# Two more dummy matmuls before the gate's transposition, the gate weights as one load, and new orders on all engines

## The chip, the core and the metric

The kernel runs on one core of one Trainium2 chip. Its engines work side by side, each through its own list of instructions in a fixed order: TensorE (PE, matmuls; PEld is its loading of weights), VectorE (DVE), ScalarE (ACT), GpSimd (POOL) and SyncE (SP, which here only issues DMAs). They wait for each other through semaphores. The metric is the time of one execution in device microseconds, as the median of several runs.

## The reference

Two branches work on the same input x of 2048 rows and 448 columns (the second branch ignores its own input), and a gate per row mixes them.

```python
g = sigmoid((x * gate_w).sum(-1))                  # one number per row
# A: attention, 16 heads of 28, four segments of 512 rows, causal within a segment,
#    plus a linear memory of the segments before (phi(t) = t+1 for t>0, else exp(t))
q, k, v = x@wq, x@wk, x@wv
o = sigmoid(beta) * (phi(q)@M)/(phi(q)@z + 1e-6) + (1-sigmoid(beta)) * softmax(q k^T * scale + mask) @ v
a = o @ wo
# B: an MLP over the rows
h = layernorm(x)
u = gelu(einsum("bsd,sf->bdf", h, w1) + b1)        # 1792 wide
b = transpose(einsum("bdf,fs->bds", u, w2) + b2)
out = g*a + (1-g)*b
```

## The kernel before

All five engines get their work from one list of operations with dependences (`Sched`). The order in which each engine takes them does not come from the program text but from a table, `ORDER`: one string of names for each engine, in which `u1-3*2` stands for two operations (step 3 and 4 of MLP group 1) and `@5` for the PSUM bank or buffer that an operation takes. `plan` only replays these strings. So an engine whose next operation isn't ready holds back everything behind it in its string, SP's DMA issues too.

The stages, in the names of the table:

- Loads. SP issues x transposed in four blocks of 512 rows (`dtx0_0` for the first three column groups, `dtx0_1` for the fourth), the weights of K and Q (`ldwk`, `ldwq`), x in rows in four pieces (`ldx0`, `ldx4`, `ldx8`, `ldx12`), beta, and the MLP weights in quarters (`ldw1_0_0` and so on). ACT's queue issues V's weights (`ldwv`), the gate's weights (`ldgw`, `ldgwb`), the last quarter of K's and the biases.
- Start of PE. `warm` is a run of dummy matmuls on ones (L626) that nothing reads. `gtr` (L810) transposes the gate's weights, which lie as rows in the zeroed `gstage`, into a column by a matmul with columns of the identity; DVE copies the column beside V's weights (`gw`, L812), so that the V projection makes the gate's sum as its 449th column. `warm2` is one more dummy. Then come V's projections of the first block (`pra`, `prb`, `lot`, `prt`: the four column groups of 128 rows of weights; the fourth overlaps the third, and its new half is done as a pair of half-row matmuls, `lo`), then K's and Q's (`pra0_`, `lok`, `prk`, `prx`, `loq`, `prq`). K's weights go through DVE first, which spreads 28 columns of a head to 32 (`padk`, `padx`, L637). `btr` (L857) transposes the biases.
- Copies out of PSUM (`cpv` L790/L792, `cpk` L706/L708, `cpq` L766/L768, `gt` L793 for the gate), on ACT or DVE as the table says.
- Layernorm on DVE: `bns` (L882, statistics of one tile of 128 rows), `bna` (L884), `vpe` (L889), `rstd` on POOL (L891), `nmr` (L893), `ln` (L898, the normalised tile).
- Attention: 40 score groups `sc` (L939) into the four PSUM banks 0 to 3, each followed by one exponential over all four on ACT (`exp`, L948); the next group can start only when the exponential has read the banks. POOL masks, `pv` (L975) multiplies with V, and DVE transposes and combines.
- MLP: `u0-0` to `u13-15` (first matrix, 16 steps over the row tiles; step t of any `u` reads `ln` of tile t and a quarter of `w1`), gelu in `gsq`, `gvh`, `garg`, `gth`, `gelu`; `y0-0` to `y15-13` (second matrix). `wo` is the output projection, `ag` its copy with the gate, `fin` (L1079) the mix, `out` the store. PE uses the `u` and `y` steps to fill the time between score groups. Most matmuls of L264 run either as one of 128 columns of weights or as four of 32 side by side.

The four banks 4 to 7 serve everything else; `@` in PE's string says which.

The dummies and the gate before:

```python
warm_up(7, "warm", -1)
warm_up(1, "warm2", P_PROJ + 0.01, 3500.0)
```

Of the kernel before, what the change touches and what calls it, by code (L numbers as in the profile page):

```python
# [5 lines left out]
ACT = mybir.ActivationFunctionType  # L6
# [12 lines left out]
NCT = 4  # L19
# [260 lines left out]
def pool_cost(n):  # L280
# [7 lines left out]
warm gtr@4 warm2 pra0@5 pra1@6 pra2@7 pra3@4 prb3 prb2 prb0 prb1 lot2 lot0 prt1 prt3 prt2 prt0 pra0_1 pra0_2 pra0_0  # L288
btr@5 lok0_0 lok0_2 prk0_0 prx0_3 prk0_2 prk0_1 loq1_2@74 loq1_0@65 prq1_2h prq1_1 prq1_2 prq1_0 loq0_0 lok1_0@57
prk1_1 prq0_0 loq0_2 lok1_2@64 prk1_0 prx1_3 prk1_2 prq0_2 prq0_2h prq0_1 lot4@75 lot6@46 prt7 prt6 prt4 prt5 sc0_0  # L290
lok2_2@64 prx2_3 u1-0@7 u0-0@5 u1-1 prk2_2 u1-2 u0-1 u1-3*2 u0-2*4 u1-5 sc0_1 lok2_0@46 prk2_1 u1-6*2 prk2_0
u2-0@6*2 sc0_2 u2-2 u0-6 u2-3 u1-8*2 u0-7 u2-4 u0-8*3 u2-5 sc0_3 u1-10 u0-11*3 u2-6 u0-14 u1-11 u0-15 u2-7*2 u1-12
u2-9 sc0_4 u1-13 u2-10 u1-14 u2-11 u4-0@4*2 u1-15 u4-2 pv0@5 u4-3 sc1_0 u2-12 u4-4 u2-13 u3-0@5*2 u2-14 u4-5 u3-2
u4-6 u3-3*2 u2-15 pv1@7 u3-5*2 u4-7 u3-7 sc1_1 u4-8*2 u3-8 u4-10 u6-0@7 u5-0@6 u4-11 u5-1 u6-1*2 u3-9 u4-12*3 u3-10
u4-15 u3-11 u6-3*3 sc1_2 u3-12*2 u5-2 u6-6*2 u3-14 u7-0@4 u3-15 u6-8*4 u5-3 u7-1 u6-12*4 u7-2 sc1_3 u5-4 u7-3*2
u5-5*3 u8-0@5 u5-8*2 u7-5 u8-1 u5-10*3 u7-6 sc1_4 u8-2 u7-7 u5-13 u8-3 pv2@7 u7-8 u8-4 u5-14 u8-5 u7-9 u5-15 u7-10
sc2_0 u8-6 mst0@7 u8-7*3 u7-11 u8-10 u9-0@6 u8-11 u9-1 sc2_1 u8-12*2 u9-2 u8-14*2 u9-3 pv3@7 u9-4 u7-12*2 u9-5
u7-14 u9-6 u7-15 u9-7 sc2_2 loq2_0@75 u9-8*2 prq2_1 u9-10*2 prq2_0 sc2_3 loq2_2@45 prq2_2 u9-12*2 wo2@7 u9-14
prq2_2h u9-15 sc2_4 mem4@4 wo0#1@7 wo3@5 pv4@6 wo1@4 sc3_0 lot8@75 prt9 u10-0@6*2 prt8 u10-2*2 sc3_1 u10-4*2 mem5@4
pv5@5 u10-6*5 sc3_2 u10-11 u11-0@4 u10-12 u11-1 u10-13*3 mst1@5 u11-2*4 sc3_3 lot10@75 u11-6*3 prt11 u11-9 prt10  # L300
u13-0@6 sc3_4 u11-10*2 mem6@5 u13-1 u11-12 pv6@7 u11-13 u13-2 u12-0@5 u11-14*2 u13-3 sc4_0 u12-1 u13-4*3 u12-2
u13-7*2 mem7@7 u13-9 u12-3*2 u13-10 sc4_1 u12-5 u13-11*2 pv7@4 u13-13*2 u12-6 u13-15 u12-7*3 sc4_2 lok3_0@74
u12-10*3 prk3_0 u12-13*3 prk3_1 sc4_3 lok3_2@67 prx3_3 prk3_2 loq3_0@45 prq3_0 sc4_4 prq3_1 wo6@6 wo7@7 sc5_0 wo5@4
wo4@6 pv8@7 y2-0@5*2 sc5_1 y2-2 y1-0@4 y2-3*2 y1-1 pv9@6 y2-5 y1-2 mem8@7 sc5_2 y1-3 y2-6 y1-4 y0-0@6 y1-5*3 y2-7
y0-1 y1-8 mem9@7 sc5_3 y0-2*3 y1-9 y2-8 y1-10 y0-5 y2-9 y0-6 y4-0@7 y2-10 y1-11 y4-1 y0-7 sc5_4 y2-11*2 y0-8 y2-13
y1-12*2 y4-2 y0-9*3 y5-0@5 y0-12 y5-1 y4-3 sc6_0 y4-4 mem10@4 y5-2 y4-5*2 y5-3 y0-13 y5-4*2 y4-7 y5-6*3 sc6_1 y4-8
pv10@4 y5-9*2 mem11@6 y5-11*3 y4-9 y3-0@4 sc6_2 y4-10 y3-1 y4-11 y3-2 y4-12*2 pv11@6 y3-3*2 sc6_3 lot14@57 y3-5
prt15 y3-6 mst2@6 prt14 y3-7*2 sc6_4 loq3_2@67 prq3_2 y3-9 prq3_2h y6-0@5 y3-10*2 y6-1 y3-12 lot12@67 sc7_0 y3-13
prt12 prt13 y6-2*3 mem12@4 sc7_1 y6-5 wo10@6 y6-6 wo8@4 pv12@7 y8-0@6 y6-7 y8-1*3 wo11@4 y8-4 mem13@7 y6-8 y8-5
sc7_2 y6-9 pv13@4 y7-0@7 y6-10 y8-6*2 y6-11*3 y8-8*2 mem14@4 sc7_3 y8-10 y7-1*2 wo9@5 pv14@4 y7-3 sc7_4 y7-4 y9-0@5  # L310
y8-11*3 y9-1 y7-5 y9-2 y11-0@4 y7-6 y9-3*2 y7-7 y9-5 y7-8 y9-6 y7-9 y9-7 y7-10 y9-8 pv15@6 y11-1 y7-11*2 y9-9*3
mem15@6 y11-2*6 y7-13 y9-12*2 y10-0@6*4 y11-8 y10-4*4 y11-9 y10-8*3 y11-10*4 y10-11*3 wo12@7 wo15@5 wo13@6 wo14@4
y13-0@7*2 y12-0@5 y13-2 y12-1 y15-0@6 y12-2*2 y14-0@4*2 y12-4 y13-3*2 y12-5*3 y14-2*4 y12-8 y13-5 y15-1 y14-6 y15-2
y14-7*3 y13-6*2 y14-10 y15-3*2 y14-11 y15-5*2 y13-8*3 y14-12 y13-11 y12-9 y14-13 y12-10 y15-7 y13-12*2 y15-8 y12-11
# [892 lines left out]
```

## Time and profile before

| | us |
|---|---|
| median of 3 runs (lowest, highest) | 173.28 (172.91, 173.67) |
| the profiled execution, as timed | 173.6 |
| its span, first to last instruction | 171.9 |
| PE busy | 167.2 |
| DVE busy | 143.9 |
| ACT busy | 128.0 |
| POOL busy | 61.5 |

The page of the profile gives busy time by engine and the chain of work that ended last; the timeline gives instructions in order of time, equal neighbours merged into one row (start, duration from the first start to the last end, count, and in brackets the idle time before and what ended it). A matmul's duration has the time in it that its results need to come out, so that neighbours overlap; how fast PE runs is read from the distance of the starts, or from the count in a stretch (the windows view: stretch, its length, PE's busy time and count, granted clock, DMA share, GB/s). The DMA view gives, for the issues in a stretch, the time from issue to landing.

### The profile page before, as it was taken

The numbers are of one execution on the slowest core, as the hardware profiler recorded it, in microseconds if no ns is written. First come the engines' busy times: TensorE is split into PE (matmuls) and PEld (weight loads), VectorE is DVE, ScalarE is ACT, GpSimd is POOL, SyncE is SP. The second block draws the span as 40 slices with busy tenths as digits, with TensorE's granted clock in tenths as the row PEclk, the third lists the DMA queues.
The fourth block names the chain that finished last, engine by engine and source line by source line (L and its number), as shares of the span: only waits on it lengthen the run. The fifth ranks groups of instructions, "written<-read, shape, count | busy, mean of one in ns | idle before, by whom it ended". The sixth has DMA issues, their size and how long they took to land.

```text
span 171.9 us, 5808 instructions
## 1 busy us (share of the span) xinstructions
PE 167.2 (97%) x2460; PEld 81.0 (47%) x2467; DVE 143.9 (84%) x327; ACT 128.0 (74%) x158; POOL 61.5 (36%) x94
## 2 busy tenths in 40 slices
PE   7899999999999999999999999999999999999994
PEld 2334434445444554546454335444554655555563
DVE  3069998848899898999999989999999999998024
ACT  0247997999999999989999999985987889001100
POOL 5000226074126325038365561537743462500000
PEclk9999999999999999999999999999999999999999
DMA  6999986997698706145028177026147351553603
GB/s 139 254 264 290 234 205 120 273 276 157 183 187 216 196 10 180 30 98 143 4 73 246 50 229 154 10 46 177 39 149 204 96 154 42 153 174 105 188 4 107
DMA packets 52585, 25.16 MB, mean 146 GB/s; under 512 B 17088, under 2 KB 52320, under 8 KB 52560
## 3 DMA queue, kind: packets, MB, share of 16 engines
q1 hardware_dynamic: 51772, 24.22, 55.0%
q10 hardware_dynamic: 788, 0.58, 1.8%
q8 instruction: 19, 0.31, 0.8%
q14 instruction: 6, 0.05, 0.1%
HBM read 18.76 MB, written 2.36 MB: 123 GB/s over the span
## 4 chain that ended last, share of the span: by engine, by line
PE 92%; ACT 5%; issue 1%; DVE 0%
PE t L264 76%; PE t L939 8%; PE t L975 5%; PE t L626 2%; ACT t L768 1%; ACT t L790 1%; ACT t L720 1%; PE t L824 1%; ACT t L706 1%; ACT t L775 1%; ACT t L751 0%; DVE t L1079 0%; ACT t L793 0%; PE t L810 0%; PE t L857 0%
## 5 line engine op out<-in xcount | busy, mean ns | idle before, releaser
L264 PE MATMUL t<-t 128*32 128x448 bf16 (+8 forms) x1746 | 146.2, 349 | 0.4 <-ACT t L793 0.2
L264 PEld LDWEIGHTS t<-t 128*32 128x32 bf16 (+1 forms) x1753 | 67.0, 97 | 64.1 <-issue 15.6
L948 ACT ACTIVATE t<-t 128x2048 bf16<-128x2048 f32 x40 | 75.0, 1876 | 8.1 <-PE t L939 7.6
L951 POOL TENSOR_SCALAR_AFFINE_SELECT t<-t 128x512 bf16<-128x512 bf16 x64 | 43.4, 694 | 47.1 <-ACT t L948 46.1
L1006 POOL TENSOR_TENSOR t<-t 128x448 bf16<-128x448 f32 x9 | 11.3, 1256 | 18.9 <-DVE t L1004 9.2
L1079 DVE SCALAR_TENSOR_TENSOR t<-t 128x448 bf16<-128x448 f32 (+2 forms) x17 | 10.8, 642 | 8.6 <-PE t L264 8.0
L1033 ACT ACTIVATE t<-t 128x448 bf16<-128x448 f32 x10 | 7.2, 724 | 12.0 <-PE t L264 11.9
L939 PE MATMUL t<-t 28*128 28x512 bf16 (+3 forms) x256 | 15.8, 301 | 0.3
L991 DVE STREAM_TRANSPOSE t<-t 128x512 f32<-128x512 f32 x16 | 11.4, 710 | 1.2 <-PE t L975 0.8
L891 POOL TENSOR_TENSOR t<-t 128x4 f32<-128x4 f32 x4 | 4.3, 1068 | 21.9 <-DVE t L889 17.4
L975 PE MATMUL t<-t 128*32 128x512 bf16 (+3 forms) x256 | 11.5, 299 | 0.0
L939 PEld LDWEIGHTS t<-t 28*128 28x128 bf16 x256 | 4.4, 92 | 14.6 <-ACT t L948 5.5
L1013 DVE STREAM_TRANSPOSE t<-t 128x512 bf16<-128x512 bf16 x16 | 11.0, 689 | 0.1
L1057 DVE TENSOR_SCALAR t<-t 128x448 f32<-128x448 f32 x11 | 7.3, 671 | 2.7 <-ACT t L1051 2.7
L1064 DVE SCALAR_TENSOR_TENSOR t<-t 128x448 bf16<-128x448 f32 x14 | 8.7, 622 | 1.0 <-ACT t L1062 1.0
L790 ACT ACTIVATE t<-t 128x448 bf16<-128x448 f32 x12 | 6.4, 550 | 3.9 <-PE t L264 3.9
L975 PEld LDWEIGHTS t<-t 128*32 128x32 bf16 x256 | 6.9, 97 | 5.1 <-DVE t L989 0.2
L882 DVE BATCH_NORM_STATS2 t<-t 128x6 f32<-128x448 bf16 x16 | 9.1, 610 | 0.0
L1051 ACT ACTIVATE t<-t 128x448 f32<-128x448 f32 x14 | 8.9, 635 | 0.3 <-PE t L264 0.2
L1002 DVE SCALAR_TENSOR_TENSOR t<-t 128x448 f32<-128x448 f32 x12 | 9.0, 750 | 0.1
L1059 DVE SCALAR_TENSOR_TENSOR t<-t 128x448 f32<-128x448 f32 x14 | 8.8, 629 | 0.3 <-ACT t L1054 0.2
L989 DVE STREAM_TRANSPOSE t<-t 128x512 f32<-128x512 f32 x12 | 8.4, 703 | 0.2
(69 smaller groups left out, 132.4 us busy)
## 6 DMA issues: line engine op xcount, KB each, us to landing
t<-in_B_w_dram SPq DMA_DIRECT2D x52, 256.0 KB, 3.6
t<-in_A_x_dram SPq DMA_DIRECT2D x4, 448.0 KB, 5.3
out_dram<-t SPq DMA_DIRECT2D x15, 112.0 KB, 2.7
t<-in_B_w_dram SPq DMA_DIRECT2D x8, 128.0 KB, 3.3
t<-in_A_wv_dram ACTq DMA_DIRECT2D x4, 112.0 KB, 4.0
t<-in_A_wo_dram SPq DMA_DIRECT2D x4, 98.0 KB
t<-in_A_wq_dram SPq DMA_DIRECT2D x1, 336.0 KB, 4.9
spare_heads<-t SPq DMA_DIRECT2D x8, 32.0 KB
```

The lines of the kernel that those rows point to most:

```text
L264: last = e.matmul(out[q], w[:, q], x, skip_group_check=True, **kw)
L882: op("DVE", lambda e: e.bn_stats(st6[:, t, :], xh[:, t, :]), reads=[R_x[t]], writes=[R_st6[t]], name=f"bns{t}", cost=512, prio=P_PROJ - 10 ...
L939: last = e.matmul(bank(hl)[:, c0 : c0 + w], kT[r, hg, s * 512 + j * 128 : s * 512 + j * 128 + 128], qT[r, hg, s * 512 + 128 * j : s * 512 ...
L948: op("ACT", lambda e: e.activation(pslot(g), ps[:, 0:4, :], ACT.Exp, scale=SCALE), reads=R_bank[0:4], writes=[g.res], take=g, name=f"exp{p ...
L951: op("POOL", lambda e, c0=c0: e.affine_select(pslot(g)[:, :, c0 : c0 + 128], pslot(g)[:, :, c0 : c0 + 128], pattern=[[0, 4], [1, 128]], co ...
L975: last = e.matmul(bank(cb)[32 * hl : 32 * hl + 32, 128 * j : 512], vaug[:, 4 * s + j, 32 * h : 32 * h + 32], pslot(P_fill[u // 2][f])[:, h ...
L991: dv(lambda e: e.transpose(t2[:, 0, :], bank(cb)[:, 0:512]), [bres(cb)], [R_tt[tb][0]], "ta", 630, use=(cb,))
L1002: dv(lambda e: e.scalar_tensor_tensor(n3[0], n3[0], oc, rb[0], op0=ALU.mult, op1=ALU.mult), [R_tt[tb][0], R_rec[tb], R_omcol], [R_tt[tb][0 ...
L1006: op("POOL", lambda e: e.tensor_tensor(o3, n3[0], n3[1], op=ALU.add), reads=R_tt[tb], writes=[R_ob[tb]], name=f"o{u}", cost=1280, port=Tru ...
L1013: dv(lambda e: e.transpose(oT[:, hg, s * 512 : s * 512 + 512], o), [R_ob[tb]], qres(hg, s), "ot", 635)
L1051: op("ACT", lambda e: e.activation(gg[:, q, :], bank(b)[:, 0:D], ACT.Square, bias=b1s[:, ft : ft + 1], scale=math.sqrt(GC)), **buse(b), re ...
L1079: op("DVE", lambda e: e.scalar_tensor_tensor(outst[:, p, c0:c1], bank(b)[:, 0 : c1 - c0], omg[:, T : T + 1], ag(T)[:, c0:c1], op0=ALU.mult ...
```

## The change

The dummy run ahead of the gate's transposition has nine matmuls instead of seven. The gate's 448 weights, before two loads into `gstage` (three rows of 128, and one row that starts at 320), come as one load of six rows of 128 that start 64 apart; rows 0, 2, 4 and 5 are the four that are used, and the transposition takes them with two matmuls, of 3 and of 1 column. All five strings of `ORDER` are new. 23 operations change their engine, most of them between ACT and DVE (copies out of PSUM, `gvh`, `ag`; two adds between POOL and DVE).

```diff
@@ ORDER
-warm gtr@4 warm2 pra0@5 pra1@6 pra2@7 pra3@4 prb3 prb2 prb0 prb1 lot2 lot0 prt1 prt3 prt2 prt0 pra0_1 pra0_2 pra0_0
-btr@5 lok0_0 lok0_2 prk0_0 prx0_3 prk0_2 prk0_1 loq1_2@74 loq1_0@65 prq1_2h prq1_1 prq1_2 prq1_0 loq0_0 lok1_0@57
...
+warm gtr@4 warm2 pra0@5 pra1@6 pra3@7 pra2@4 prb2 prb3 prb0 prb1 lot0 lot2 prt2 prt3 prt1 prt0 pra0_1 pra0_2 pra0_0
+lok0_0 prk0_0 prk0_1 btr@4 lok0_2 prk0_2 prx0_3 loq0_0 loq1_2@67 loq1_0@45 prq1_0 prq1_2h prq1_2 prq1_1 loq0_2
...
@@ build_kernel
-    op("ACT", lambda e: e.dma_start(gstage[0:3, :], GW[0:384].rearrange("(c p) -> c p", p=128)),
-       writes=[R_gst[0]], name="ldgw", dma=True, prio=-3, cost=500, nbytes=2000)
-    op("ACT", lambda e: e.dma_start(gstage[3:4, :], GW[320:448].rearrange("(c p) -> c p", p=128)),
-       writes=[R_gst[1]], name="ldgwb", dma=True, prio=-3, cost=500, nbytes=2000)
+    gview = bass.AP(GW.tensor, GW.offset, [[64, 6], [1, 128]])
+    op("ACT", lambda e: e.dma_start(gstage[0:6, :], gview), writes=R_gst, name="ldgw", dma=True, prio=-3, cost=500,
+       nbytes=2000)
...
-    warm_up(7, "warm", -1)
+    warm_up(9, "warm", -1)
...
-        op("PE", lambda e: e.matmul(gps(), gstage[:, :], ident[:, 0:NCT], start=True, stop=True, skip_group_check=True),
+        def fn(e):
+            e.matmul(bank(b)[:, 0:3], gstage[:, :], ident[:, 0:5:2], start=True, stop=True, skip_group_check=True)
+            return e.matmul(bank(b)[:, 3:4], gstage[:, :], ident[:, 5:6], start=True, stop=True, skip_group_check=True)
+
+        op("PE", fn,
            reads=R_gst + [R_ident], writes=[bres(b)], name="gtr", mode="f", cost=60, prio=P_PROJ - 1, take=b)
```

The rest of the table moves in the same way; three places of the new order are shown in the prediction. For a reader who wants to follow the names there, two stretches of other strings, before and after:

```
DVE before: ... nmr0 bna4 bna6 ln2 bna7 bns11 vpe4 ln0 bns8 bns10 bna9 ln1 bna8 bna11 bna10 bns15 nmr4 bns14 ln5 ln3 ...
DVE after:  ... bns8 bns11 bna9 bns10 cpq0_2 nmr4 nmr0 bns14 bna8 ln1 ln6 ln3 bna14 ln0 ln7 ln2 ln4 bna10 bna11 ln5 ...
SP before:  ... ldx0 ldx4 ldx8 ldbeta ldw1_0_0 dtx2_0 ldx12 dtx2_1 ldw1_0_1 ldw1_1_0 ldw1_0_2 tk0_0 ...
SP after:   ... ldx0 ldx4 ldx8 dtx2_0 dtx2_1 ldx12 ldbeta ldw1_0_0 ldw1_0_1 ldw1_1_0 ldw1_0_2 tk0_0 ...
```

More of the change, by code (lines that the diff above doesn't have):

```diff
@@ L293 @@
[L293 to L302, printed above, removed]
@@ new lines @@
+y15-7#1 y15-8#1 y15-9#1 y15-10#1 y15-11#1 y15-12#1 y15-13#1""",
+    "ACT": """
+ldwv0 ldgw ldwv1 ldwv2 ldwvb ldwkb ldb1 ldb2 gt2 cpv1 cpv0 gt1 gt3 cpk0_0 ek0_0 gt0 cpk0_3 cpk0_2 cpq0_3 cpq1_0
+cpq1_2 cpq1_2#1 cpq1_1 cpk1_0 ek0_1 cpk1_2 cpk1_3 cpq1_3 eq1_2 cpk1_1 cpq0_1 cpq0_0 eq1_0 cpv7 cpv6 gt7 cpq0_2#1
+gt6 cpv5 cpv4 gt5 gt4 exp0_0@2 cpk2_3 cpq2_3 cpk2_2 tb exp0_1@3 ek0_2 exp0_2@4 eq1_1 exp0_3@0 gsq0 exp0_4@1 gsq1
+gth0 exp1_0@5 gsq2 ek0_3 gvh2 exp1_1@6 gth2 eq1_3 ek1_0 gsq4 gth1 exp1_2@2 gth4 gsq3 ek1_1 exp1_3@3 gsq6 gth3 gvh6
@@ new lines @@
+gcol3 eps14 phq3_3 o13 ta14 fin8 rec14 oa14 om14 ta15 ot13 tm15 omg3 eps15 rec15 om15 oa15 ot14 fin7 ot15 fin9
+fin10 b2g3 fin11 fin14 fin13 fin12 fin15 fin15#1""",
+    "POOL": """
+szg oo0 v0 og0 og1 szb id0 id1 v1 oo1 oo2 og2 mhalf rstd0 rstd4 rstd8 rstd12 mask0_2_2 mask0_1_1 mask0_2_2#1
+mask0_0_0 mask0_3_0 mask0_1_3 mask0_4_1 mask0_4_3 mask1_1_1 mask1_2_2 mask1_2_2#1 mask1_3_0 mask1_1_3 mask1_0_0
+mask1_4_1 mask1_4_3 mask2_2_2 mask2_1_1 mask2_1_3 mask2_2_2#1 mask2_0_0 mask2_3_0 mask2_4_1 mask2_4_3 mask3_0_0
```

120 lines of the change are left out of this document (60 added, 60 removed).

## The prediction

> **What bounds the kernel now.** I read the page first (busy shares, chain of waits), then the timeline of the start, then who is late where.
>
> ```profile
> span 171.9 us, 5808 instructions
> PE 167.2 (97%) x2460; PEld 81.0 (47%) x2467; DVE 143.9 (84%) x327; ACT 128.0 (74%) x158; POOL 61.5 (36%) x94
> PE 92%; ACT 5%; issue 1%; DVE 0%
> L264 PE MATMUL t<-t 128*32 128x448 bf16 (+8 forms) x1746 | 146.2, 349 | 0.4 <-ACT t L793 0.2
> ```
>
> TensorE (PE) is busy 97% of the span, the chain that ends last is 92% PE, and the 1746 projection and MLP matmuls have 0.4 us of idle time before them in all. A new order on the other engines has nothing to win in the middle of this kernel; it can only let a wait in. What is left to win stands at the start.
>
> ```profile
> 0.83 3.14 PE L626 MATMUL t<-const-bfloat16-1.0 128*128 128x512 bf16 x7 [0.83 <-PEq L1192]
> 4.75 0.16 PE L810 MATMUL t<-t 128*128 128x4 bf16 x1 [0.78 <-issue]
> 5.27 6.48 PE L264 MATMUL t<-t 128*128 128x449 bf16 x22
> 11.63 0.17 PE L857 MATMUL t<-t 128*128 128x30 bf16 x1
> 11.74 0.93 PE L264 MATMUL t<-t 64*128 64x512 bf16 x5
> ...
> 4.72 0.10 PEld L810 LDWEIGHTS t<-t 128*128 128x128 bf16 x1 [1.66 <-issue]
> 10.30 0.96 PEld L264 LDWEIGHTS t<-t 128*128 128x128 bf16 x5
> ...
> 4.95 0.17 DVE L812 CAST t<-t 128x4 bf16<-128x4 f32 x1 [2.56 <-PE t L810]
> ```
>
> Seven dummy matmuls run from 0.83, then PE stands still for 0.95 us (0.83 + 2.93 = 3.76 to 4.72) until the gate's transposition (L810) gets its data; one more dummy, and the projections start at 5.27. At what rate do they run? The windows view counts matmuls in equal stretches.
>
> ```profile
> 0.83:3.76 2.93, 2.93 (x7) 1.00 0.74 168
> 5.27:9.57 4.30, 4.30 (x14) 1.00 1.12 289
> 9.92:14.10 4.18, 4.18 (x24) 1.00 1.04 273
> ```
>
> A 512-column dummy takes 2.93/7 = 0.42 us; the five loads at 10.30 are 0.215 apart, so the same width takes half. 14 matmuls fit into 4.30 us before 9.57, and 24, mostly wider ones, into 4.18 us after 9.92. The column of the granted clock says 1.00 throughout, but the pitch says PE runs at half rate up to about 9.7 and at full rate after. The first burst of 2.93 us did not bring the full rate; the unbroken run from 4.75 did, after about 5.0 us.
>
> [...]
>
> **The change, part by part.** *Dummies and gate load.*
>
> ```profile
> 1.20 0.74 ACTq L531 DMA_DIRECT2D t<-in_gate_w_dram  x1
> 1.97 0.24 ACTq L533 DMA_DIRECT2D t<-in_gate_w_dram  x1
> ```
>
> L810 waits for both gate loads; the second is issued 0.77 us after the first. As one load, issued at 1.20, the data should be there by about 4.72 - 0.77 = 3.95. Nine dummies end at 0.83 + 9 x 0.42 = 4.6, so the hole is gone and the transposition (now two matmuls of 3 and 1 columns instead of one of 4) runs at 4.6; the projections start at 5.27 - 0.12 = 5.15. Work is then unbroken from 0.83. By the rows the full rate comes between 0.83 + 2.93 = 3.8 (too short in the first burst) and 0.83 + 5.0 = 5.8; were the release not moved, 9.7 (a rival).
>
> The 16 matmuls of 449 columns took from 5.27 to 10.30. At full rate they need 449/512 x 0.215 = 0.19 each; the four half-row ones among them run two at a time between two changes of form at 0.105 (below), so 14 x 0.19 + 0.2 = 2.9 us. With the release at 5.8, half of the 0.65 us before it is lost, and they end at 5.15 + 2.9 + 0.3 = 8.4. But the K projection behind them waits for padded weights.
>
> ```profile
> 8.49 0.47 DVE L637 COPY t<-t 128x784 bf16<-128x784 bf16 x2 [3.36 <-DMA t<-in_A_wk_dram]
> 10.12 0.62 DVE L792 CAST t<-t 128x448 bf16<-128x448 f32 x1 [1.16 <-PE t L264]
> 10.66 0.80 DVE L637 COPY t<-t 128x392 bf16<-128x392 bf16 x6
> ```
>
> VectorE (DVE) waits for the K weights until 8.49 and is done with the first two pads at 8.96. That load is untouched, so with 0.04 for a hand-over between engines (L810 ends at 4.91, its copy starts at 4.95) the K projection cannot start before 9.0: **this, not the clock, is the new bound**, and any release up to about 7 gives the same. [...] The other four pads stood at 10.66 because the value copy ahead of them waited for PE; with PE earlier they are done by about 10.1. Six matmuls of 512 columns (6 x 0.215 = 1.29) from 9.0 and one change of form, and the half-row pair that stood at 11.74 starts at 10.4: **-1.34 us**.
>
> *PE's own order.* At the start of PE's program (L626/L625 dummies, L810 gate, L264 projections, L857/L860 bias transposition), before and now:
>
> ```order
> L626 MATMUL t<-const-bfloat16-1.0 128x512 x7
> L810 MATMUL t<-t 128x4
> L626 MATMUL t<-const-bfloat16-1.0 128x512
> L264 MATMUL t<-t 128x449 x16
> L264 MATMUL t<-t 128x512 x6
> L857 MATMUL t<-t 128x30
> ```
> ```order
> L625 MATMUL t<-const-bfloat16-1.0 128x512 x9
> L810 MATMUL t<-t 128x3
> L811 MATMUL t<-t 128x1
> L625 MATMUL t<-const-bfloat16-1.0 128x512
> L264 MATMUL t<-t 128x449 x16
> L264 MATMUL t<-t 128x512 x10
> L860 MATMUL t<-t 128x30
> ```
>
> The bias transposition moved behind the first half-row pair and parts it from the second, so PE changes its form of tiling twice more.
>
> ```profile
> 29.09 0.40 PE L939 MATMUL t<-t 28*128 28x384 bf16 x8
> 29.41 0.39 PE L264 MATMUL t<-t 64*128 64x512 bf16 x2
> ```
>
> A score group of 512 columns (384 + 128) holds PE 0.32 us instead of 0.215: 0.105 for a change of form. Counted through both tables there are 107 such changes for 105, so **+0.21 us**. The number of streamed columns stays; the tail (last output half, its copy, its store) has the same last steps: 0.
>
> *Normalisation and x loads.* SP's queue before and now (L521 transposing x loads, L506 plain x loads, L540/L539 beta, L562/L561 MLP weights):
>
> ```order
> L506 DMA t<-in_A_x_dram 128x4x448 x3
> L540 DMA t<-in_A_beta_dram 128x16
> L562 DMA t<-in_B_w_dram 128x4x256
> L521 DMA_TRANSPOSE t<-in_A_x_dram 128x3x512
> L506 DMA t<-in_A_x_dram 128x4x448
> L521 DMA_TRANSPOSE t<-in_A_x_dram 128x1x512
> L562 DMA t<-in_B_w_dram 128x4x256 x3
> ```
> ```order
> L506 DMA t<-in_A_x_dram 128x4x448 x3
> L521 DMA_TRANSPOSE t<-in_A_x_dram 128x3x512
> L521 DMA_TRANSPOSE t<-in_A_x_dram 128x1x512
> L506 DMA t<-in_A_x_dram 128x4x448
> L539 DMA t<-in_A_beta_dram 128x16
> L561 DMA t<-in_B_w_dram 128x4x256 x4
> ```
>
> The last x load goes behind both transposing loads, the first MLP weights behind it. On DVE, the stretch in which the first tiles are normalised, before (L882 statistics, L884 their sums, L889 and L893 coefficients, L898 normalised tiles) and now (L885, L887, L892 and L896, L901):
>
> ```order
> L893 SCALAR_TENSOR_TENSOR t<-t 128x4
> L884 BN_AGGR t<-t 128x2 x2
> L898 TENSOR_SCALAR t<-t 128x448
> L884 BN_AGGR t<-t 128x2
> L882 BN_STATS t<-t 128x6
> L889 TENSOR_SCALAR t<-t 128x4
> L898 TENSOR_SCALAR t<-t 128x448
> L882 BN_STATS t<-t 128x6 x2
> ```
> ```order
> L885 BN_STATS t<-t 128x6
> L765 CAST t<-t 128x256
> L896 SCALAR_TENSOR_TENSOR t<-t 128x4 x2
> L885 BN_STATS t<-t 128x6
> L887 BN_AGGR t<-t 128x2
> L901 TENSOR_SCALAR t<-t 128x448 x3
> L887 BN_AGGR t<-t 128x2
> L901 TENSOR_SCALAR t<-t 128x448 x4
> ```
>
> Before, tiles 2 and 0 (the two L898) were normalised between statistics of earlier loads. The second L885 of the new rows is tile 14, of the last x load, and stands ahead of the normalised tiles 1, 6, 3, 0 in DVE's fixed order. The first MLP matmul (u0-0) needs tile 0 and the first weights.
>
> ```profile
> 11.46 0.50 SPq L540 DMA_DIRECT2D t<-in_A_beta_dram  x1
> 12.01 0.55 SPq L562 DMA_DIRECT2D t<-in_B_w_dram  x1
> 12.60 4.68 SPq L521 DMA_TRANSPOSE t<-in_A_x_dram  x1
> 17.33 0.58 SPq L506 DMA_DIRECT2D t<-in_A_x_dram  x1
> 17.95 1.18 SPq L521 DMA_TRANSPOSE t<-in_A_x_dram  x1
> 19.18 1.68 SPq L562 DMA_DIRECT2D t<-in_B_w_dram  x3
> ...
> t<-in_A_x_dram SPq DMA_DIRECT2D x1, 448.0 KB, 4.3
> t<-in_A_x_dram SPq DMA_DIRECT2D x1, 448.0 KB, 5.5
> t<-in_B_w_dram SPq DMA_DIRECT2D x1, 256.0 KB, 5.3
> ...
> 17.09 0.36 DVE L884 BATCH_NORM_AGGREGATE t<-t 128x2 f32<-128x6 f32 x4
> 17.37 1.12 DVE L882 BATCH_NORM_STATS2 t<-t 128x6 f32<-128x448 bf16 x2
> 18.41 0.15 DVE L889 TENSOR_SCALAR t<-t 128x4 f32<-128x4 f32 x1
> 24.42 1.00 DVE L898 TENSOR_SCALAR t<-t 128x448 bf16<-128x448 bf16 x3
> ...
> 25.64 3.51 PE L264 MATMUL t<-t 128*128 128x512 bf16 x17 [0.16 <-ACT t L793]
> ```
>
> When is u0-0 due? The first MLP matmul stood second in the last row, about 26.1, and one projection of three matmuls stands between it and the half-row pair ahead in both orders; 1.1 earlier it is due at 25.0. DVE's work: the first x load lands at 9.74 + 4.3 = 14.05 as before; from there to the end of normalised tile 0 stand 13 statistics at 0.52 ((18.41 - 17.37)/2), 11 sums at 0.07 ((17.37 - 17.09)/4), four normalised tiles at 0.32 and about 1.2 us of small ones: 10.1 us, done at 24.1 if nothing waits. Tile 14 waits for the last x load: behind it come 0.6 + 0.07 + 3 x 0.32 + 0.07 + 0.4 = 2.0 us, so u0-0 stays on time if that load lands by 22.9. It landed at 17.33 + 5.5 = 22.8 before. Now the large transposing issue starts 1.1 us earlier; it ends between 16.2 (its 4.68 us kept) and 17.3 17.3 (held back to the same end), plus 1.18: issue at 17.3 to 18.5, landing at 22.8 to 24.0; less up to 0.9 us, as the 256 KB of MLP weights are no longer ahead (289 GB/s in the window row). Wait at u0-0: 0 to 1.2 us. The MLP weights, two issues (1.1) behind, land at 23.7 to 24.9, under the same bound. I take **+0.1 us**, the near end, as the smaller load ahead speaks for it.
>
> *The other reorderings* (evacuations swapped between ScalarE (ACT) and DVE, gathers, stores) are costed at nothing. Their cover is PE's work between two score groups, while ACT makes the exponentials:
>
> ```profile
> 25.51 1.87 ACT L948 ACTIVATE t<-t 128x2048 bf16<-128x2048 f32 x1
> 29.54 1.88 ACT L948 ACTIVATE t<-t 128x2048 bf16<-128x2048 f32 x1 [0.93 <-PE t L939]
> ```
>
> Before the second exponential ACT waits 0.93 us for PE, so PE may come earlier by that much. One more key copy stands behind the first exponential now (0.62 by the value copy above). If the first stayed at 25.51 while PE comes 1.1 us earlier, ACT would be late by 1.1 - 0.93 + 0.62 = 0.8 us: bound 0 to +0.8, taken as 0, since ACT's first copies start earlier with PE's first results.
>
> Sum: -1.34 + 0.21 + 0.1 = **-1.03 us**. The profiled execution took 173.6 (span 171.9, 1.7 around it), so 172.6 by its own time; it stands 0.3 above the runs' median of 173.28. From the median: **172.3**, its own range 171.6 to 172.8.
>
> **Rivals.** *The clock does not come earlier* (the release is tied to something other than unbroken work): PE starts 0.12 earlier and pays 0.21 + 0.1: 173.5. For it: nothing but that one execution is shown; against: the first burst failed and the longer one did not. *The gain is given back at u0-0*, waits of 0.6 to 1.3 us, by the upper bounds above: 172.8 to 173.5. *The slower side: the last x load lands late.* Place: DVE's statistics of tile 14 ahead of tile 0, for which u0-0 waits. Each us beyond 22.9 costs one; at 24.0 the gain is gone, from 24.9 on the kernel is slower by over 0.5%. What could do it:
>
> ```profile
> 21.00:22.00 1.00, 1.00 (x8) 1.00 1.24 48
> 22.00:23.00 1.00, 1.00 (x8) 1.00 0.38 94
> ```
>
> In these two microseconds the DMA moved 48 and 94 GB/s instead of the 273 of 9.92 to 14.10. If the load meets a second such hole: landing at 25.0, a wait of 2.1, 173.28 - 1.13 + 2.1 = 174.3. Against it: the load had that hole in its 5.5 us already.
>
> **How the numbers follow.** Forecast 0.56, no earlier clock 0.11, given back 0.15, slower 0.18. A difference of 0.5% (0.87 us) is what a measurement of this kernel can tell: 172.41 or less is faster, 174.15 or more is slower. Of the forecast's 0.56 I put 0.10 between 172.41 and 172.8: faster 0.46, within 0.5% 0.10 + 0.11 + 0.15 = 0.36, slower 0.18. The range takes in the two middle cases and the near part of the slower one: 171.6 to 174.0.
>
> **What would show it.** Right: in the windows view some 20 matmuls between 5.2 and 9.5; the K projection starting at the end of the second pad, near 9.0; the half-row pair near 10.4; no idle time above 0.2 us before L264 at 24 to 26. Wrong: half the pitch up to 9 (clock); a gap before the first MLP matmul ended by DVE L901 or a load of x or MLP weights; score groups released by ACT with PE idle.

## The result, and the profile after

The changed kernel is slower: 174.09 us in the median of 20 runs (173.55 to 174.91), beside 172.97 (172.21 to 173.72) for 20 runs of the kernel before on the same chip. The ratio is 1.0062, with a 95% interval from 1.0044 to 1.0080: 1.1 us lost, where 1.0 was forecast to be won. The profiled execution does not show this by its length: it took 173.63 us (before 173.6), at the low end of its runs, while before's lies at the high end of its own. Medians, ratios and counts here leave out the executions that took over 1.5% longer than the fastest of their kernel (among them four of e7's six, and the profiled ones of e8 and f2).

The page of the kernel after, its first rows and the chain that ended last:

```profile
span 171.8 us, 5790 instructions
PE 167.5 (98%) x2455; PEld 82.1 (48%) x2455; DVE 143.0 (83%) x326; ACT 128.8 (75%) x159; POOL 63.3 (37%) x94
PE 85%; DMA 7%; DVE 3%; ACT 1%; issue 1%; POOL 1%; ACTq 1%; POOLq 0%
L942 PE MATMUL t<-t 28*128 28x512 bf16 (+3 forms) x256 | 15.9, 301 | 0.5 <-ACT t L951 0.5
```

The chain was 92% TensorE; now it is 85%, and 7% are DMA. The score groups (L942, L939 before) had 0.3 us of idle time before them in all, put down to no engine; now it is 0.5, ended by ScalarE. Those are the two things to follow. First the start, the timeline of TensorE and its weight loads, and the windows view of the two stretches that the prediction used:

```profile
0.82 4.00 PE L625 MATMUL t<-const-bfloat16-1.0 128*128 128x512 bf16 x9 [0.82 <-PEq L1195]
4.62 0.21 PE L810 MATMUL t<-t 128*128 128x3 bf16 x1
5.21 2.03 PE L264 MATMUL t<-t 128*128 128x449 bf16 x7
7.68 3.14 PE L264 MATMUL t<-t 64*128 64x449 bf16 x16 [0.26 <-DMA t<-in_A_wv_dram]
9.03 0.98 PEld L264 LDWEIGHTS t<-t 128*128 128x128 bf16 x6 [0.36 <-DVE t L636]
10.43 0.10 PEld L264 LDWEIGHTS t<-t 64*128 64x128 bf16 x2 [0.42 <-DVE t L636]
...
5.27:9.57 4.30, 4.04 (x20) 1.52 (x20) 1.06 (x4) 1.16 (x2) 0.00 (x0) 1.00 1.14 297
9.92:14.10 4.18, 4.18 (x25) 1.50 (x24) 3.28 (x13) 3.51 (x10) 0.00 (x0) 1.00 1.08 268
```

The hole is gone, 20 matmuls for 14 fit between 5.27 and 9.57, the K projection starts at 9.03 behind the padding of its weights (L636), and the half-row pair stands at 10.43 (11.73 before). The forecast of the start holds to a few hundredths in this execution. The prediction's estimate from before's rows was that the full rate comes between 3.8 and 5.8; here the pitch of the 449s falls from 0.374 to 0.19 at 6.3 to 6.4 (starts at 5.91, 6.28, 6.50, 6.70), about 3.4 us ahead of before's 9.7 and well ahead of the K projection. The moment differs from execution to execution: in other profiles of kernels without the hole the rate rose anywhere from 3.65 to 6.7.

Then the two places where TensorE waits later: score group sc5_4, and y12-0 near the end (timeline rows of ScalarE, TensorE and VectorE). Some names: `ek`, `mk` and `phk` are the three steps of phi(k) (the exponential on ScalarE, then two steps on VectorE), `tk` its transposition by DMA, `eq` the exponential of phi(q), `gk` and `gq` the moves of parts of K and Q by way of DRAM (`spare_heads`), `mst` and `mem` the matmuls of the linear memory.

```profile
108.34 1.88 ACT L951 ACTIVATE t<-t 128x2048 bf16<-128x2048 f32 x1 [0.89 <-PE t L942]
111.09 0.63 ACT L750 ACTIVATE t<-t 128x512 bf16<-128x512 bf16 x1 [0.88 <-DMA t<-t]
111.63 1.86 ACT L951 ACTIVATE t<-t 128x2048 bf16<-128x2048 f32 x1
113.54 0.40 PE L942 MATMUL t<-t 28*128 28x384 bf16 x8 [0.53 <-ACT t L951]
...
156.90 0.68 DVE L1082 SCALAR_TENSOR_TENSOR t<-t 128x448 bf16<-128x448 f32 x1 [0.78 <-DMA out_dram<-t]
```

ScalarE stands at `ek2_3` (L750) until the DMA transposition of keys `tk2_1` has landed, since `ek2_3` writes into the buffer that `tk2_1` reads (there are two, taken in turn; the expectations below call `ek2_3` a copy). The exponential of the scores is queued behind it; so that is late, and the score group that reuses its banks waits 0.53 us. At 156.90 `fin11` waits for the store `out7` that still reads its buffer, and y12-0 (157.73) for the bank that `fin11` empties.

`tk2_1` lands 3.2 us later than before: VectorE finishes its data at 107.08 (105.25 before), and the transfer takes 4.0 us from issue to landing (2.6 before), which I did not follow. It is not the only late one. The windows view of before (first three rows) and after, 20 us each; the last two columns are the DMA's share and GB/s:

```profile
80.00:100.00 20.00, 19.89 (x306) 9.09 (x300) 19.66 (x41) 19.92 (x24) 11.91 (x15) 1.00 0.34 97
100.00:120.00 20.00, 19.85 (x222) 9.24 (x219) 18.56 (x40) 16.94 (x16) 8.75 (x13) 1.00 0.45 115
120.00:140.00 20.00, 19.85 (x408) 10.60 (x405) 19.27 (x38) 17.42 (x20) 10.71 (x14) 1.00 0.47 140
```
```profile
80.00:100.00 20.00, 20.00 (x238) 8.73 (x227) 19.52 (x36) 20.00 (x26) 9.64 (x12) 1.00 0.52 132
100.00:120.00 20.00, 19.47 (x249) 9.15 (x251) 18.08 (x38) 16.63 (x15) 10.19 (x13) 1.00 0.16 45
120.00:140.00 20.00, 20.00 (x385) 10.21 (x374) 19.18 (x40) 16.04 (x19) 10.35 (x14) 1.00 0.60 166
```

From 100 to 120 the DMA carries 45 GB/s where it carried 115; then 166 for 140. SP's timeline after shows what it stands at:

```profile
93.47 3.15 SPq L561 DMA_DIRECT2D t<-in_B_w_dram  x6
107.11 1.20 SPq L757 DMA_TRANSPOSE t<-t  x1
108.35 0.58 SPq L561 DMA_DIRECT2D t<-in_B_w_dram  x1
115.56 0.36 SPq L1086 DMA_DIRECT2D out_dram<-t  x1
```

SP stands from 96.6 to 107.1 at `tk2_1`, until its data is there, and from 108.9 to 115.6 at the first store. Behind them in its fixed order stand loads and gathers that need neither. What this left of slack, from the landings in the two traces (us between landing and the first user's start):

| transfer -> user | before | after |
|---|---|---|
| `tk2_1` -> `ek2_3` | 107.90 -> 110.09: 2.19 | 111.07 -> 111.09: 0.02 |
| `ldw2_3_0` -> `y6-0` | 118.09 -> 129.27: 11.18 | 128.03 -> 128.23: 0.21 |
| `gk3_h1` -> `sc7_2` | 116.55 -> 138.58: 22.03 | 138.38 -> 138.78: 0.40 |
| `gq3_h0` -> `sc7_2` before, `eq3_3` after | 136.03 -> 138.58: 2.55 | 138.58 -> 138.60: 0.02 (`sc7_2`: 138.78, 0.20) |
| `out7` -> `fin11` | 157.11 -> 157.13: 0.03 | 156.87 -> 156.90: 0.02 |

### The profile page after: what moved, and what is told of

It is laid out like the page before. It is cut to its first block, busy times and chain, and to the rows that moved or that the text cites. A ratio compares the mean times of both kernels' runs of the same rounds, so it can differ in the third digit from the quotient of the medians.

```text
span 171.8 us, 5790 instructions
## 1 busy us (share of the span) xinstructions
PE 167.5 (98%) x2455; PEld 82.1 (48%) x2455; DVE 143.0 (83%) x326; ACT 128.8 (75%) x159; POOL 63.3 (37%) x94
## 4 chain that ended last, share of the span: by engine, by line
PE 85%; DMA 7%; DVE 3%; ACT 1%; issue 1%; POOL 1%; ACTq 1%; POOLq 0%
PE t L264 72%; PE t L942 7%; PE t L978 5%; DMA t<-in_A_wv_dram 3%; DMA t<-t 2%; DMA out_dram<-t 2%; ACT t L951 1%; DVE t L1082 1%; PE t L827 1%; DVE t L992 1%; ACTq L511 1%; DVE t L1005 0%; ACT t L750 0%; DVE t L1016 0%; DVE t L754 0%
## 5 line engine op out<-in xcount | busy, mean ns | idle before, releaser
L264 PE MATMUL t<-t 128*32 128x448 bf16 (+7 forms) x1738 | 144.7, 348 | 0.4 <-DMA t<-in_A_wv_dram 0.3
L264 PEld LDWEIGHTS t<-t 128*32 128x32 bf16 (+1 forms) x1738 | 67.8, 97 | 63.1 <-issue 13.1
L954 POOL TENSOR_SCALAR_AFFINE_SELECT t<-t 128x512 bf16<-128x512 bf16 x64 | 45.8, 729 | 50.8 <-ACT t L951 43.4
L942 PE MATMUL t<-t 28*128 28x512 bf16 (+3 forms) x256 | 15.9, 301 | 0.5 <-ACT t L951 0.5
L1036 ACT ACTIVATE t<-t 128x448 bf16<-128x448 f32 x9 | 6.5, 726 | 11.9 <-DVE t L911 9.9
L942 PEld LDWEIGHTS t<-t 28*128 28x128 bf16 x256 | 4.5, 92 | 14.7 <-ACT t L951 6.2
L1062 DVE SCALAR_TENSOR_TENSOR t<-t 128x448 f32<-128x448 f32 x14 | 8.5, 609 | 0.0
L779 DVE SCALAR_TENSOR_TENSOR t<-t 128x512 bf16<-128x512 bf16 x12 | 8.4, 700 | 0.0
L1005 DVE SCALAR_TENSOR_TENSOR t<-t 128x448 f32<-128x448 f32 x12 | 8.4, 698 | 0.0
```

The lines of the kernel that those rows point to most:

```text
L264: last = e.matmul(out[q], w[:, q], x, skip_group_check=True, **kw)
L942: last = e.matmul(bank(hl)[:, c0 : c0 + w], kT[r, hg, s * 512 + j * 128 : s * 512 + j * 128 + 128], qT[r, hg, s * 512 + 128 * j : s * 512 ...
L954: op("POOL", lambda e, c0=c0: e.affine_select(pslot(g)[:, :, c0 : c0 + 128], pslot(g)[:, :, c0 : c0 + 128], pattern=[[0, 4], [1, 128]], co ...
```

## The experiments

Theory 1: the early gain is there in every execution, and the new orders lose it and 1.1 us more in such late transfers. Theory 2: in a part of its executions the kernel before reaches the full rate early too, so that the hole costs less in the median than in its profile. The expectations call this the clock opening; what is measured is the pitch, while the granted clock reads 1.00 in every window of before and after above, and what brings the rise was not shown. Ratios are to runs of the kernel before made on the same chip along with them.

**Each half alone.** e1: the early part with the orders of before. e2: the orders of after with the early part undone. And both kernels again for a second profile.

```diff
 e1 (against after)
-ORDER of after
+ORDER of before, without ldgwb
 e2 (against after)
-    warm_up(9, "warm", -1)
+    warm_up(7, "warm", -1)
+ two gate loads, one transposing matmul, as before
```

> The kernel before with the early part of the change alone: nine dummies, one gate load, two transposing matmuls; the orders of all engines as before. Theory 1 (the early gain of about 1.2 us is there in every execution, and the new orders lose it and 1.1 more later, in waits for late DMAs): 1.2 below before, 171.6 to 172.1, the half-row pair (first rows of 64 on TensorE) at 10.4, and no TensorE stall over 0.3 after 30 us. Theory 2 (before's clock also opens early in a part of its executions, so the hole costs less in the median than in its profiled execution): within 0.5 below before, 172.4 to 172.9. Either way it must be faster than after by over 1.

> The kernel after with the early part undone: seven dummies, two gate loads, one transposing matmul; the orders of all engines as after. Theory 1: the late waits of after stay or shrink by a few tenths, the early gain is gone: 1.8 to 2.6 above before, 174.8 to 175.5. Theory 2: as much as after, 173.9 to 174.4.

> The kernel before once more, for a second profiled execution. Theory 1: TensorE at half rate up to about 9.7 as in the first profile, 172.5 to 173.7, and the same waits. Theory 2: if this execution is one of the faster ones (172.2 to 172.7), its full rate starts about 3.4 us earlier, and its half-row pair stands near 10.5 and not near 11.7.

> The kernel after once more, for a second profiled execution; its first one, at 173.6, was among its fastest. If this one is near the median (174.1 to 174.9), theory 1 expects the 0.5 to 1.2 more in TensorE waits for DMAs that had next to no slack in the first profile: before score group sc7_2 (Q and K gathers of the fourth segment), before y6-0 (second MLP weights), at sc5_4 (key transposes) or at y12-0 (output stores). A rival: the full rate starts at another time than 6.3 and the early part is longer.

Measured: e1 172.78 us, 0.9978 [0.9953, 1.0003]; e2 175.36, 1.0132 [1.0097, 1.0167]; before again 173.9, after again 174.65. So the orders cost, and the early part wins. e2 fits theory 1; e1's 0.4 us fit theory 2 and not theory 1, although its profiled execution (172.45) was 1.15 shorter than before's first. The second profile of after has the wait at sc5_4 again (0.6) and new ones; TensorE's waits (us in total, times, longest) and one row each of ScalarE's and TensorE's timeline:

```profile
PE t L942 <- DMA t<-spare_heads: 0.6, 1, 0.6
PE t L942 <- ACT t L951: 0.6, 1, 0.6
PE t L827 <- DMA t<-t: 0.2, 1, 0.2
...
139.62 0.63 ACT L774 ACTIVATE t<-t 128x512 bf16<-128x512 bf16 x1 [0.97 <-DMA t<-spare_heads]
139.80 0.40 PE L942 MATMUL t<-t 28*128 28x256 bf16 x8 [0.62 <-DMA t<-spare_heads]
```

sc7_2 waited here for the Q and K gathers (`spare_heads`) that had landed with 0.20 and 0.40 to spare in the first profile, and `mst1` (L827) for the key transposes. That is the 1.0 us between the two executions, as theory 1 had it.

**An account that closes.** For every profile I took the starts of the first K projection and of the last four matmuls, which run side by side, and summed the TensorE waits between them (start to start, less what the matmuls and changes of form need; waits under 0.06 left out):

| kernel (profiled time) | K projection starts | to the last matmuls | waits in it | rest |
|---|---|---|---|---|
| before (173.6) | 10.30 | 158.98 | 0 | 158.98 |
| before again (173.9) | 10.34 | 159.22 | 0.23 | 158.99 |
| e1 (172.45) | 9.01 | 158.97 | 0 | 158.97 |
| e5, below (172.22) | 8.81 | 158.95 | 0 | 158.95 |
| after (173.63) | 9.03 | 160.02 | 0.92: sc5_4 0.59, y12-0 0.32 | 159.10 |
| after again (174.65) | 9.01 | 161.06 | 2.01: mst1 0.38, sc5_4 0.63, sc7_2 0.69, y12-0 0.31 | 159.05 |
| after, third (174.38) | 8.83 | 160.92 | 1.80: sc5_4 0.66, y6-0 0.45, y12-0 0.69 | 159.11 |
| e2 (175.83) | 10.04 | 161.05 | 1.99: mem11 0.78, y6-0 0.60, y12-0 0.61 | 159.06 |

The rest is the same to 0.16 us. So all that the new orders lose after the start, but for 0.1, is TensorE waiting, and nothing of it is slower work. Against e5, the median of after is 1.0062/0.9959 = 1.0103 or 1.8 us longer; its three profiles hold 0.9, 1.8 and 2.0 us of waits.

**The early part again, and with eight output buffers for four.**

```diff
 e6 (against e1)
-    outst = sb([128, 4, D])
+    outst = sb([128, 8, D])
...
-        p = T % 4
+        p = T % 8
```

> The early part alone, once more (the same kernel as e1), since 172.78 against 173.1 left 0.32 +- 0.4 open, while its profiled execution was 1.2 to 1.4 shorter than the two of before. Theory 1: the gain is whole, 0.8 to 1.3 below before. Theory 2 (before's clock opens early in a part of its executions): 0.2 to 0.5 below before.

> The early part alone, with eight output buffers for four. Theory 1: before's order has the wait of fin11 for out7 too (0.04 of wo14 in its first profile, 0.23 in its second): 0.0 to 0.3 below the early part alone. Rival: no change, since in e1's profile no such stall is left.

Measured: e5 172.56, 0.9959 [0.9940, 0.9979]; e6 172.52, 0.9959 [0.9939, 0.9979]. The gain is real, 0.7 us, between the ranges of the two theories and about half of the 1.4 by which the profiles differ (173.6 and 173.9 against 172.45, 172.22 and 172.42), and the buffers bring nothing. e6's start shows something more:

```profile
0.82 3.47 PE L625 MATMUL t<-const-bfloat16-1.0 128*128 128x512 bf16 x9 [0.82 <-PEq L1195]
4.13 0.17 PE L810 MATMUL t<-t 128*128 128x3 bf16 x1
```

Nine dummies took 3.31 us (0.82 to 4.13) and not 9 x 0.42 = 3.8: the rate rose at about 3.65, after 2.8 us of work (6.7 dummies at 0.42 and 2.3 at 0.215 make 3.31), less than before's first burst of 2.93. Its first seven dummies are those of before, so a burst like that can be followed by the full rate.

**The number of dummies in the kernel before.** Eight and five for seven, nothing else.

```diff
-    warm_up(7, "warm", -1)
+    warm_up(8, "warm", -1)   (e9)
+    warm_up(5, "warm", -1)   (e10)
```

> The kernel before with eight dummies for seven ahead of the gate's transposition, nothing else. [...]

> The kernel before with five dummies for seven. [...]

Measured: e9 172.96, 0.9984 [0.9959, 1.0010]; e10 173.94, 1.0039 [1.0011, 1.0066], with a lowest time of 173.19 where before's was 172.48. TensorE's start in e9 and in e10:

```profile
0.82 3.57 PE L626 MATMUL t<-const-bfloat16-1.0 128*128 128x512 bf16 x8 [0.82 <-PEq L1192]
5.65 0.16 PE L810 MATMUL t<-t 128*128 128x4 bf16 x1 [1.26 <-issue]
```
```profile
0.82 2.29 PE L626 MATMUL t<-const-bfloat16-1.0 128*128 128x512 bf16 x5 [0.82 <-PEq L1192]
5.25 0.16 PE L810 MATMUL t<-t 128*128 128x4 bf16 x1 [2.14 <-DMA t<-in_gate_w_dram]
```

In both TensorE waits for the gate's second load in any case, so two dummies fewer can cost time only through TensorE's rate. They cost 0.7 us [0.2, 1.1], so before reaches the full rate earlier than e10 in a part of its executions: by its burst alone, as in e6, or because its hole is shorter; e10 doesn't part these. That is theory 2, and more than my estimate of 0.2 to 0.6. For e9 my estimate was the gain of the early part alone, 0.5 to 0.9; it came to 0.3 us, within its interval. Its profile has a hole of about 1.5 us (4.2 to 5.65) and not 0.53 (before's 0.95 less one dummy of 0.42), since TensorE could go on after the second gate load only at 5.65 (4.75 and 4.72 in before's profiles, 5.25 in e10), so it doesn't test a shorter hole. None of the profiles caught an execution of before with an early rise of the rate; that it happens rests on e6 and e10.

**Taking the waits out of after.** e3 takes four out at once, e4 only those of the gathers and of one quarter of the second MLP weights.

```diff
 e4 = SP's string of after with
-gq3_h1 ldw2_5_2 gq3_h2 ldw2_4_3 gk3_h1 gq3_h0 ldw2_4_1 out3
+gk3_h1 gq3_h1 gq3_h0 gq3_h2 ldw2_4_1 ldw2_4_3 ldw2_5_2 out3
 (and ldw2_3_0 changed places with ldw2_3_2)
 e3 = e4, eight output buffers, and
-ACT: exp5_2@4 ek2_3 exp5_3@5 exp5_4@6
+ACT: exp5_2@4 exp5_3@5 ek2_3 exp5_4@6
-DVE: mk2_3 rec9 om8 phq2_2 gcol2 oa8 om9
+DVE: rec9 om8 phq2_2 gcol2 oa8 mk2_3 om9
```

> The kernel after with four late transfers taken off TensorE's way: ScalarE takes the exponential exp5_3 ahead of the copy ek2_3 that waited for the key transposes, SP issues the last Q and K gathers and one quarter of the second MLP weights earlier, and eight output buffers stand for four. Theory 1 (late transfers make the loss): the two profiles of after hold 0.59 + 0.32 and 0.63 + 0.68 + 0.21 us of such stalls, so 0.9 to 1.5 less than after: 172.6 to 173.2, not slower than before by over 0.3. Rival (the loss is in something that every execution of after has, such as two more changes of form or a slower start): at most 0.4 less than after, 173.7 or more.

> The kernel after with the last Q and K gathers and one quarter of the second MLP weights issued earlier on SP, nothing else. Theory 1: the wait before sc7_2 is there in a part of after's executions only (0 and 0.68 in its two profiles), so the median falls by 0.2 to 0.6, to 173.5 to 173.9, and the highest time by more. Rival: no change.

Measured: e3 174.01, 1.0048 [1.0016, 1.0080]; e4 173.87, 1.0043 [1.0017, 1.0069]. Neither is told from after, and e3's 0.9 to 1.5 us did not come. e3's profile (175.05) has none of the four waits, and 2.41 us of others: u7-0 1.22, sc1_3 0.26, pv10 0.55, mem11 0.37. The first follows from ScalarE's queue again, in e3's timeline:

```profile
48.13 0.63 ACT L748 ACTIVATE t<-t 128x512 bf16<-128x512 bf16 x1 [0.84 <-DMA t<-t]
48.66 0.62 ACT L1052 ACTIVATE t<-t 128x448 f32<-128x448 f32 x1
...
50.05 0.74 PE L264 MATMUL t<-t 128*128 128x448 bf16 x3 [1.06 <-DVE t L1058]
```

`ek1_0` (L748) waits for a transposition until 48.13, where it ran at 46.14 in after; the first step of the gelu (L1052) is queued behind it, VectorE's part (L1058) behind that, and the bank that u7-0 takes comes free a microsecond late.

**One string alone.** e7 has SP's string of after in e1, e8 SP's string of before in after.

> The early part alone (e5) with one string of the change more: SP's, so the DMAs stand in after's order and all engines that compute in before's. Theory 1a (SP's new order makes the late transfers): most of the 1.8 us between early alone and after, 173.6 to 174.4, with stalls before mst1, y6-0 or sc7_2. Theory 1b (the new orders on ScalarE and VectorE make data later, and the DMAs of it with them): within 0.4 of early alone, 172.3 to 173.0. A mismatch of the strings could add waits of its own; they would show as other places than those of after.

> The kernel after with before's string on SP. Theory 1a: 1.0 to 1.8 below after, 172.4 to 173.2, without the stalls at sc7_2 and y6-0. Theory 1b: as after, 173.8 or more, with the stall at sc5_4 (key transposes behind VectorE's phk2_1) and at y12-0.

Measured: e7 178.3, in two executions; e8 179.8, 1.0353 [1.0300, 1.0405]. Both are far slower than either kernel, so they don't part theory 1a from 1b: an order of transfers fits only the orders of the engines that make and use the data. e7's profile (178.35) has 6.0 us of waits in the stretch of the table, the two largest at other places than after's (2.2 before lot14, 2.3 before y8-4).

**The waits one by one.** f1: only ScalarE's swap, with `mk2_3` behind `om9`. f2: f1 and eight buffers. f3: f2 and the SP edits of e4.

> The kernel after once more, as the base of the three that follow: 0.6% (1.1 us) above before. In its profile the waits at sc5_4 (about 0.6) and y12-0 (about 0.3) again, and the stretch from the first K projection to the last matmul at 159.06 us plus the waits (159.06 in all four profiles of these orders so far, 158.97 for the old ones).

> After, with ScalarE's exponential exp5_3 ahead of the copy ek2_3, and on VectorE the step that reads that copy (mk2_3) behind om9. Theory (the wait at sc5_4 is half of the loss): 0.5 to 0.7 below after. Rival (the wait moves on to the next thing that is late, as in e3): within 0.3 of after, with a new stall of some 0.5 between 114 and 123.

> f1 with eight output buffers for four, so that fin11 needn't wait for the store out7. Theory: 0.2 to 0.4 below f1, 0.8 to 1.0 below after, no stall before y12-0. Rival: the 0.3 is given back at the next bank, no change against f1.

> f2 with the last Q and K gathers and a quarter of the second MLP weights earlier on SP. Theory: 0.1 to 0.4 below f2 in the median, 1.0 to 1.3 below after, so about level with before; what then still parts it from the early part alone (0.5 or so) are waits that come and go. Rival: these waits wander elsewhere, no change against f2.

Measured: after 174.38, 1.0073 [1.0036, 1.0111]; f1 174.19, 1.0058 [1.0034, 1.0081]; f2 174.4, 1.0076 [1.0048, 1.0104]; f3 173.77, 1.0038 [1.0017, 1.0059]. In f1 the wait at sc5_4 is gone, and two stand in its place, 0.38 at pv10 and 0.37 at mem11 (0.66 at sc5_4 in after's third profile); sc7_2 and y12-0 wait on, 0.55 and 0.39. f1 and f2 came out as their rivals had it: the wait moves on. Rows of VectorE, GpSimd and TensorE in f1, and the last two of VectorE as they stand in after:

```profile
113.89 1.23 DVE L751 TENSOR_SCALAR t<-t 128x512 bf16<-128x512 bf16 x1
...
116.23 1.03 DVE L1004 SCALAR_TENSOR_TENSOR t<-t 128x448 f32<-128x448 f32 x1
...
118.89 1.02 DVE L753 SCALAR_TENSOR_TENSOR t<-t 128x512 bf16<-128x512 bf16 x1
...
113.52 1.45 POOL L1008 TENSOR_TENSOR t<-t 128x448 bf16<-128x448 f32 x1 [2.39 <-DVE t L1004]
...
119.11 0.73 PE L977 MATMUL t<-t 128*32 128x512 bf16 x16 [0.31 <-DVE t L1081]
```
```profile
116.03 0.68 DVE L1005 SCALAR_TENSOR_TENSOR t<-t 128x448 f32<-128x448 f32 x1
...
118.34 0.68 DVE L754 SCALAR_TENSOR_TENSOR t<-t 128x512 bf16<-128x512 bf16 x1
```

The moved step (L751, 0.29 us in after) took 1.23 here, to 115.12; GpSimd's add beside it ran from 113.52 to 114.97. What stretched the step was not shown. Two more VectorE steps, one ahead of pv10 (L1004) and one ahead of mem11 (L753), took 1.03 and 1.02 us where after's took 0.68.

**The last two.** g1: the SP edits of e4, ScalarE's swap, and `mk2_3` two steps further, past that add. g2: the same with eight buffers.

> After, with the last gathers and a quarter of the second MLP weights earlier on SP, exp5_3 ahead of ek2_3 on ScalarE, and mk2_3 on VectorE behind fin2, where the GpSimd add is over. Theory (the loss is these waits, and this time none is made): no stall over 0.2 at sc5_4, pv10, mem11, sc7_2 and y6-0, the one at y12-0 (0.3 to 0.7) left: 0.7 to 1.1 below after's 174.2, so 173.1 to 173.5, level with before. Rival (whatever is taken out comes back at another place, since the engines that feed TensorE have no slack in these orders): 173.8 or more, with new stalls that add up to over 1 us. The stretch from the first K projection to the last matmul is 159.06 us plus the stalls in either case.

> g1 with eight output buffers for four. If eight buffers only take the wait at y12-0 away: 0.2 to 0.5 below g1, 172.7 to 173.3. If they are what makes the wait before u7-0 (0.8 to 1.3 in e3, f2 and f3): not below g1, and that wait in the profile.

Measured: g1 174.15, 1.0059 [1.0024, 1.0095]; g2 173.52, 1.0023 [0.9990, 1.0055]. g1 missed its theory's 173.1 to 173.5 and fits its rival. The profiles hold 0.94 us (pv10 0.38, mem11 0.37, y12-0 0.19) and 0.75 us (pv10 0.38, mem11 0.38), and rests of 159.05. The moved step takes 0.64 there, so its 1.23 beside that add is not what makes pv10 and mem11 wait. With sc5_4 0.6 earlier, VectorE's results for them (the mix and a transposition) are the next to be late. In all five profiles with the new ScalarE order the two steps ahead of them take 1.02 to 1.05 us where after's three have 0.67 to 0.68; the 0.35 of each is about the size of the two waits. GpSimd is at work beside them, but that this stretches them was not tried. Eight buffers do not bring the wait at u7-0 every time: g2 is without it, e3 and f3 have it (1.22 and 0.76), and none of the seven with four buffers; whether they are its cause is open.

Counted over ten profiles of the new orders (after three times, e2, e3, e4, f1, f3, g1, g2), the edits do what they say at their own place. The waits at sc7_2 or y6-0 are in four of the five profiles without the SP edits (after again and f1; e2 and after, third) and in none of the five with them. The one at y12-0 is in all seven with four buffers and in none of the three with eight. The one at sc5_4 is in four of the five with the old ScalarE order; in all five with the new one pv10 and mem11 wait instead, 0.75 to 0.93 us. In time, only g2 with all edits is no longer told from before, and none reaches the early part alone.

## Why the prediction was wrong

**The start: mechanism right, size right in the profile, too large for the median.** The projections at 5.15 (5.21), the K projection at 9.0 (9.03) as the new bound, the half-row pair 1.34 earlier (1.30): these came as worked out. One wait was missed: TensorE stood 0.26 us for V's last weights (the row at 7.68), so V's projections ended near 8.95 and not at 8.4; the bound at 9.0 hid it. That TensorE's rate is not the bound held: in the other profiles with the early part the rate rose between 3.65 and 6.7, and the K projection started between 8.6 and 9.25. But the 1.34 was read off one execution of before, and carried to the median as if every execution reached the full rate as late as that one (about 9.7). The step that failed is "the first burst of 2.93 us did not bring the full rate", taken for a property of the kernel. In the median the early part is worth 0.4 (e1) to 0.7 us (e5, e6). The rival that the clock would not come earlier fell: 6.3 to 6.4 in after for 9.7 in before.

**Two more changes of form, +0.21.** In the table the new orders' rest is about 0.1 longer, 159.05 to 159.11 for 158.95 to 158.99. Small, with the right sign; that it is the changes of form was not tried.

**The wait at u0-0, +0.1, and the slower rival.** TensorE's timeline has no idle time there:

```profile
23.69 0.40 PE L942 MATMUL t<-t 28*128 28x512 bf16 x4
24.02 3.30 PE L264 MATMUL t<-t 64*128 64x512 bf16 x16
```

u0-0 started at 25.00, when it was due. (The terms behind tile 14 in the prediction add up to 2.1 us, not 2.0; its 22.9 goes by 2.1.) The slower side came, but not by this mechanism, and its 0.18 was given to the wrong place.

**"The other reorderings are costed at nothing": the step that failed.** Its cover, TensorE's work between two score groups, was shown at the first two exponentials and taken for all 40. The sentence ahead of it, that a new order "can only let a wait in", was right and was not priced. The price is 0.9 to 2.0 us in after's three profiles, in waits at sc5_4, y12-0, sc7_2, y6-0 and mst1. Before's trace held the material: its slacks (2.2, 2.6, 11 and 22 us in the table above) beside the new places in SP's string, where `gk3_h1` and `ldw2_3_0`, ahead of every store before, moved behind three, would have named the places, though not the sum. One of the prediction's own signs of being wrong came: a score group released by ScalarE while TensorE stood idle (sc5_4).

**The sum.** Early alone -0.7, orders +1.8 on top of it, together +1.1 us. Without the early part the orders cost 2.3 (e2), so the early part was worth 1.2 in the new orders; the intervals do not tell this from 0.7. In the two first profiles: -1.27 at the start, +1.04 after it, and 0.25 behind the last matmuls and around the span that I did not follow; the difference of their times is +0.03.

**What stays open.** Which of the five strings costs how much: they work only together (e7, e8). The waits that were taken out came back in part elsewhere, and not all of those were named. That before reaches the full rate early in some executions was inferred, not seen. Whether the dummies or the single gate load bring the early gain was not parted.

The fastest version of this study is the early part alone with the orders of before (e5): 0.9959 of before, 1.0% under after.

## What to carry to other kernels

Where an order is replaced as a whole, list for every transfer the slack between landing and first use, and look at what it now stands behind in its queue: a queue that parks at one unfinished piece of data (SP here from 96.6 to 107.1) holds back all that could already go. Removing one wait helps only by the slack of the next thing behind it, so sum the waits over the whole stretch, and over several executions, before believing an edit. A gain read off one profiled execution that hangs on the moment TensorE's rate rises (3.65 to 6.7 here without the hole) was worth half in the median here; time it alone.

## What was not expected of the hardware

TensorE's rate rose in an execution where it had worked only 2.8 us (e6), while 2.93 us and a hole did not do it in two profiles of before; in the kernels without the hole it rose anywhere between 3.65 and 6.7. The second of two loads of the gate's weights (0.2 KB, issued at 1.97 in before) let TensorE go on at between 4.72 and 5.65 us in the five profiles of kernels with two. And one VectorE step of 0.29 us (after) took 1.23 beside a GpSimd add of 1.45 (f1).
